# Windowed attention in plain 128-key blocks: 128x128 value products in place of 64-row pieces

## The chip, the cores and the metric

The kernel runs on one core of one Trainium2 chip. The metric is the device time of one execution in microseconds (us). A core has five engines that run side by side and wait for each other through semaphores: TensorE (PE in the profile; PEld is its row for loading the stationary operand), VectorE (DVE), ScalarE (ACT), GpSimd (POOL) and SyncE (SP). Transfers between DRAM and the on-chip memory are issued here from the queues of SP and POOL.

## The reference

Four batches of eight heads, 768 positions, 64 elements a head. Attention looks back over a window of 128 positions and always also at the first four positions (the sinks); a small expert layer then replaces 128 chosen rows of each batch.

```
scores = (q @ k.T) / 8
keep   = (pos_k < 4) | ((pos_q - pos_k >= 0) & (pos_q - pos_k < 128))
a      = softmax(where(keep, scores, -1e9))
x      = a @ v                                  # [4, 768, 512] with heads side by side
s      = x @ w_gate                             # one score a row
top    = the 128 rows of each batch with the largest s
out    = x;  out[top] = x[top] + sigmoid(s[top]) * (relu(x[top] @ w1) @ w2)
```

## The kernel before

**Units.** The attention is cut into blocks of 128 queries. A full unit is one block of one batch with all eight heads. Batches 1 to 3 have six full units each. Batch 0 is done in two halves of four heads, so it has twelve half units. That makes 30 units in all, in the list `steps`. The loop at L595 goes through them. In unit i it issues the scores of unit i+2 (`step_scores`), then the value products of unit i (`values`), then the normalisation (`norm`), and then what was hung on that unit by `at`, `late` and `before`: transposes of the keys and queries of the next batch, the scores for the sinks, ranks, the choice of rows, and the expert layer of an earlier batch. Every engine works its list in this order.

**Scores (L201 to L248).** Keys lie along the partitions of the output and queries along its columns. `scores(b, kc, gi)` makes four heads at a time: `a` chooses the head pair, `e` the head in the pair. Each block of 128 keys is made as two products of 64 keys (`m`), each with a window of 192 queries. They are 64x64 tiles of the PE array, so four of them, in different quarters of the array, can be in flight. For the second head pair (`a == 1`, heads 4 to 7) the block starts 64 keys earlier than for the first: the keys of these heads are shifted by half a block. The masks are added by more products with an identity matrix (L226, and L239, L245 at the first and last block). They touch only the two 64-column pieces of each window that are cut by the causal edge or by the window's far edge. ScalarE then takes the exponential of the 128x1024 result into a buffer `pt` (L248), in fp32.

**Values (L250 to L285).** The output has queries along the partitions and, for each head, 64 value columns plus one of ones that gives the softmax sum: 65 columns, fp32. The queries of a block are made as two halves `c`, which are the two column halves of the PE array. For each half a window of keys is covered by one product of all 128 key rows (`FULL`) and by two of 64 rows (`LO` and `HI`). So a head has two 128-row products and four of 64 rows in two array quarters each. An fp32 product is two matmul instructions in the profile, each with its own load of the stationary operand (`pt`).

**Sinks.** The four sink keys of each head are copied into `ksk` (L178). `sink_scores` (L185) makes their scores for a whole batch, for both query halves side by side, and ScalarE puts the exponential into `psk`. In `values` four products (`be`, `c`) of 64 rows, one in each array quarter, add the sinks' part (L264 to L272), with the sinks' values in `vsk`. `vsk` is filled at the start by four transfers on POOL's queue (L441), by DVE (L590), and by a copy on POOL (L592).

**Storage of the values.** There are two pairs of value buffers. In the second of a pair the keys are shifted by 64, which needs one more block. `load_v` (L140) issues two transfers a block on SP's queue, and `load_v_first` (L152) loads batch 0.

**Results of the products.** The scores alternate between two pairs of PSUM banks (`SC`). The value products of all units go to the same pair of banks (`X`), so the products of unit i+1 wait until `norm` of unit i has read it. `spread` (L312) broadcasts the scores of 128 rows by one fp32 product with a stationary operand of 128x128; it isn't touched by the change.

## Time and profile before

| | |
|---|---|
| median of 3 runs | 160.05 us (159.14 to 161.59) |
| the profiled execution, its own time | 160.06 us |
| its span, first to last instruction | 158.3 us |
| mean granted TensorE clock | 0.916 of full speed |
| busy: PE, DVE, ACT, POOL | 79%, 58%, 50%, 47% of the span |
| value products, L259 | 1440 matmuls, 48.4 us busy |
| exponentials, L248 | 48 of 128x1024, 1031 ns each |
| sink products, L269 | 180 matmuls, 15.9 us busy |
| score products, L210 | 384 matmuls, 18.4 us busy |
| mask products, L226, L239, L245 | 240 matmuls |

A line of the profile's table of groups names the source line, the engine, the operation, output<-inputs by name, the tile of the PE array (rows\*columns), partitions x elements and type of the operand, and the count; then the busy time, the mean of one in ns, and the idle time ahead of it with what ended it. A line of the timeline has the start (us from the span's start), the duration from the first start to the last end, the engine, the group and how many instructions were merged into it. Matmuls overlap and their ends are modelled, so what a product costs is read from the distance of starts and not from the duration of one. "issue" stands for idle time that ended without a releaser that the profile shows.

### The profile page before, as it was taken

The page shows a single profiled execution, that of the slowest core. Times are in us where ns is not written, and L with a number is a line of the kernel's source. Part 1 is how long each engine was busy: PE and PEld are TensorE (multiplying, and loading weights), DVE is VectorE, ACT ScalarE, POOL GpSimd, SP SyncE. Part 2 cuts the span into 40 slices and gives each one's busy share as a digit, 9 for nine tenths or more (in the row PEclk, how much of TensorE's full clock was granted, in tenths as well). Part 3 has the DMA queues.
Part 4 walks back from the last instruction along what each step waited for, and adds up shares of the span by engine and source line. Part 5 has one row for each costly group of instructions (what it writes and reads, how often), then busy time and mean ns, then how long its engine had stood idle before and what let it go on. Part 6 is the DMA issues. An engine that isn't in the chain of part 4 may idle for free. (4 is left out here: it accounts for less than half of the span.)

```text
span 158.3 us, 6368 instructions
## 1 busy us (share of the span) xinstructions
PE 125.5 (79%) x2756; PEld 95.2 (60%) x2756; DVE 91.2 (58%) x281; ACT 79.2 (50%) x106; POOL 75.1 (47%) x123
## 2 busy tenths in 40 slices
PE   6759797979499988578999997968299999889400
PEld 2236585757368867455787786756297785768100
DVE  6560344377424744129799896888982674783100
ACT  3248646559448785471878487747026642223100
POOL 8717799999399290149006046401051270602220
PEclk9965999999957999969999999999959999999975
DMA  4968979999979999799552743999440431110211
GB/s 157 300 139 276 301 256 253 391 377 368 341 173 340 324 363 331 187 268 261 172 153 59 242 136 76 187 215 229 106 133 4 137 133 70 66 70 12 86 42 60
DMA packets 36795, 30.85 MB, mean 195 GB/s; under 512 B 26896, under 2 KB 30352, under 8 KB 36768
## 3 DMA queue, kind: packets, MB, share of 16 engines
q1 hardware_dynamic: 31712, 16.79, 37.7%
q0 software_dynamic: 5056, 13.67, 28.8%
q8 instruction: 21, 0.34, 0.9%
q14 instruction: 6, 0.05, 0.1%
HBM read 25.20 MB, written 7.35 MB: 206 GB/s over the span
## 5 line engine op out<-in xcount | busy, mean ns | idle before, releaser
L259 PE MATMUL ps<-vbuf,pt 64*64 64x65 f32 (+1 forms) x1440 | 48.4, 231 | 8.0 <-issue 7.2
L259 PEld LDWEIGHTS ps<-vbuf,pt 64*64 64x64 f32 (+1 forms) x1440 | 41.2, 140 | 20.1 <-issue 16.5
L248 ACT ACTIVATE pt<-ps 128x1024 f32<-128x1024 f32 x48 | 47.3, 1031 | 6.8 <-PE ps L226 6.6
L292 DVE RECIPROCAL rz<-ps 128x8 f32<-128x8 f32 (+1 forms) x30 | 5.9, 197 | 38.1 <-PE ps L259 38.0
L138 POOL CAST kq<-raw 128x768 bf16<-128x768 f32 x28 | 23.2, 861 | 2.4 <-DMA raw<-in_q_dram 1.0
L183 POOL COPY ksk<-KT 64x4 bf16<-64x4 bf16 x32 | 7.3, 227 | 30.8 <-DVE KT L174 19.2
L210 PE MATMUL ps<-QT,KT 64*64 64x192 bf16 (+2 forms) x384 | 18.4, 258 | 2.7 <-ACT QT L176 1.7
L295 DVE TENSOR_TENSOR x<-ps,rz 128x256 f32<-128x256 f32 (+1 forms) x60 | 19.5, 366 | 1.2
L299 DVE CUSTOM_DVE_ANT_0 junk<-x,wgb 128x512 f32<-128x512 f32 x24 | 19.0, 792 | 0.4
L269 PE MATMUL ps<-vsk,psk 64*64 64x260 f32 (+1 forms) x180 | 15.9, 360 | 2.8 <-DVE x L295 2.8
L226 PE MATMUL ps<-mask,ident_b 64*64 64x256 bf16 (+1 forms) x208 | 16.5, 280 | 1.5 <-issue 1.5
L169 PE MATMUL ps<-ident_b,kq 128*128 128x128 bf16 x192 | 15.0, 231 | 2.8 <-DVE kq L138 2.4
L176 ACT COPY QT<-ps 128x768 bf16<-128x768 bf16 x16 | 12.8, 801 | 8.1 <-PE ps L169 8.1
L309 DVE TENSOR_SCALAR_CACHE_REDUCE junk<-sbc,scol 128x768 bf16<-128x768 f32 x12 | 12.1, 1012 | 6.6 <-DMA sbc<-srow 6.2
L210 PEld LDWEIGHTS <-KT 64*64 64x64 bf16 x384 | 10.7, 111 | 7.9 <-issue 4.6
L169 PEld LDWEIGHTS <-kq 128*128 128x128 bf16 x192 | 12.1, 103 | 5.2 <-DVE kq L138 3.4
L367 POOL DMA_INDIRECT xe<-out_dram,idx x4 | 4.9, 1218 | 20.8 <-DVE gt L358 15.8
L399 POOL DMA_INDIRECT out_dram<-y,idx x4 | 4.2, 1052 | 13.6 <-issue 6.4
L269 PEld LDWEIGHTS ps<-vsk,psk 64*64 64x64 f32 x180 | 7.4, 140 | 4.5 <-DVE x L295 3.2
L226 PEld LDWEIGHTS <-ident_b 64*64 64x64 bf16 x208 | 8.8, 117 | 1.7 <-issue 1.7
L174 DVE COPY KT<-ps 128x768 bf16<-128x768 bf16 x10 | 9.5, 951 | 0.1
L385 PE MATMUL ps<-xeT,w_sb 128*128 128x128 bf16 x128 | 9.1, 236 | 0.0
(84 smaller groups left out, 151.5 us busy)
## 6 DMA issues: line engine op xcount, KB each, us to landing
out_dram<-x SPq DMA_DIRECT2D x24, 256.0 KB, 4.3
raw<-in_k_dram POOLq DMA_DIRECT2D x12, 384.0 KB, 7.1
raw<-in_q_dram POOLq DMA_DIRECT2D x12, 384.0 KB, 7.8
vbuf<-in_v_dram SPq DMA_DIRECT2D x33, 128.0 KB, 5.4
w_sb<-in_moe_w_dram POOLq DMA_DIRECT2D x4, 512.0 KB, 10.4
raw<-in_k_dram SPq DMA_DIRECT2D x4, 384.0 KB, 3.4
raw<-in_q_dram SPq DMA_DIRECT2D x4, 384.0 KB, 5.5
vbuf<-in_v_dram SPq DMA_DIRECT2D x2, 384.0 KB, 7.7
```

The costliest lines, as they stand in the source:

```text
L138: (eng or pool).tensor_copy(out=o, in_=i)
L169: pe.transpose(out=trp[:, c, :], in_=src[:, c, :, :].rearrange("p h d -> p (h d)"), identity=ident_b[:, :])
L174: dve.tensor_copy(out=o, in_=i)
L176: act.copy(out=o, in_=i)
L210: pe.matmul(out=sc[64 * m:64 * m + 64, e, a, o:o + n], lhsT=s.KT[r, hp, k0:k0 + 64], rhs=s.QT[r, hp, k0:k0 + n], start=a == 0, stop=False, ...
L226: pe.matmul(out=o, lhsT=ident_b[r, r], rhs=w[r].unsqueeze(1).to_broadcast((64, a.stop - a.start, 2, 64)), start=False, stop=True, skip_gro ...
L248: act.activation(out=po[:, gi, :, :, :], in_=sc[:, :, :, :], func=ACT.Exp, scale=0.125)
L259: pe.matmul(out=ps[64 * c:64 * c + 64, bank + be, hh * SK:hh * SK + SK], lhsT=p[i][rows, h, 64 * slot:64 * slot + 64], rhs=s.v[be][rows, h ...
L269: pe.matmul(out=ps[64 * c:64 * c + 64, bank + be, a * SK:z * SK], lhsT=s.psk[which][r, c, 64 * (j - 1):64 * j], rhs=vsk[r, b, be, a:z, :], ...
L295: dve.tensor_tensor(out=xo[:, e, :, :], in0=xg[:, e, :, 0:D], in1=rz[:, e, 0:n, :].to_broadcast((128, n, D)), op=ALU.mult)
L299: dve.tensor_tensor_reduce(out=junk[:, :], in0=x, in1=wgb[:, :], scale=1.0, scalar=0.0, op0=ALU.mult, op1=ALU.add, accum_out=st[b].scol[:, ...
L309: dve.tensor_scalar(out=junk[:, :].bitcast(BF16)[:, 0:S], in0=sbc[:, :], scalar1=st[b].scol[:, c:c + 1], scalar2=0.0, op0=ALU.is_gt, op1=A ...
```

## The change

The keys are no longer shifted for heads 4 to 7, and the pieces of 64 are put together:

- Scores: one product for a head and block, 128 keys by 256 queries (128 in the last block). These are 64x128 tiles of the array. The masks are full: the four mask products of a call each cover all 256 queries of two heads, 512 columns, with zeros where nothing is masked. They stay 64x64 tiles. The special cases of the first and last block go.
- Values: two products of 128 rows for a head, with the 128 queries of the block as the stationary operand. These are 128x128 tiles. The first block of a batch has one product a head.
- Sinks: two products of 32 rows a unit, each with 128 queries. `sink_scores` writes both pieces to the same 64 partitions, where before two lay side by side on 128.
- `vsk` has half its columns, is filled by eight transfers on POOL's queue, and the copy of L592 goes; the selections for `own4` on POOL go from two to four.
- One value buffer of eight heads a batch: one transfer a block. The exponential of the last block has half the columns.

The core of the diff:

```diff
+    vbuf = [one([128, H, NB, VS], FP32, f"vbuf{i}") for i in range(2)]
+    vsk = one([64, B, HP, SK], FP32, "vsk")
+    mask = one([128, 3, 4, 64], BF16, "mask")
...
     def load_v(b, c):
...
+        return sp.dma_start(out=st[b].v[:, :, c, 0:D], in_=v[b, :, c * 128:(c + 1) * 128, :].rearrange("h p d -> p h d"))
...
     def sink_scores(b, hps, which, bank):
         s = st[b]
         for hp in hps:
...
-            for c in range(2):
-                o = 64 * (g ^ c)
-                q2 = s.QT[:, hp, 128:S].rearrange("p (j c n) -> p j c n", c=2, n=64)[:, :, c, :]
-                pe.matmul(out=ps[o:o + 64, bank + c, 0:320], lhsT=s.ksk[:, hp, :], rhs=q2,
-                          start=hp == mine[0], stop=hp == mine[-1], skip_group_check=True)
...
+            for n in range(2):
+                pe.matmul(out=ps[0:64, bank + n, 0:320], lhsT=s.ksk[:, hp, :], rhs=s.QT[:, hp, 128 + 320 * n:448 + 320 * n],
+                          start=hp == hps[0], stop=hp == hps[-1], skip_group_check=True)
...
     def scores(b, kc, gi):
...
-            for m in range(2):
-                k0 = kc * 128 - 64 * a + 64 * m
-                if k0 >= 0:
-                    for e in range(2):
-                        score(m, e, a, k0, 64 * m, min(W3, S - k0))
...
+            hp = 2 * a + gi
             for e in range(2):
...
+                r = slice(64 * e, 64 * e + 64)
+                pe.matmul(out=sc[:, e, a, 0:n], lhsT=s.KT[r, hp, k0:k0 + 128], rhs=s.QT[r, hp, k0:k0 + n],
+                          start=a == 0, stop=False, skip_group_check=True)
         for m in range(2):
             for e in range(2):
                 r = slice(64 * e, 64 * e + 64)
...
+                w = mask[r, 2 if kc == 0 and m == 0 else m, 0:n // 64, :].rearrange("p t n -> p (t n)")
+                pe.matmul(out=sc[64 * m:64 * m + 64, e, :, 0:n], lhsT=ident_b[r, r],
+                          rhs=w.unsqueeze(1).to_broadcast((64, 2, n)), start=False, stop=True, skip_group_check=True)
...
     def values(b, j, heads, bank, which):
...
+        if j:
+            for be in range(2):
+                r = slice(32 * be, 32 * be + 32)
+                pe.matmul(out=ps[:, bank + be, a * SK:z * SK], lhsT=s.psk[which][r, 128 * (j - 1):128 * j],
+                          rhs=vsk[r, b, a:z, :], start=True, stop=False, skip_group_check=True)
         for hh in heads:
...
+            for be in range(2):
+                h = 4 * be + hh
+                for i in ((j - 1, j) if j else (j,)):
+                    q0 = 128 * (j - i)
+                    pe.matmul(out=ps[:, bank + be, hh * SK:hh * SK + SK], lhsT=ptn[(b, i)][:, h, q0:q0 + 128],
+                              rhs=s.v[:, h, i, 0:SK], start=j == 0 and hh == a, stop=False, skip_group_check=True)
...
-        for hh in range(HP):
-            r0 = NSINK * hh
-            pool.dma_start(out=vsk[r0:r0 + NSINK, :, :, hh, 0:D].rearrange("p b e d -> p (b e) d"), in_=v4[hh, 0:NSINK])
+        for h in range(H):
+            r0 = 32 * (h // 4) + NSINK * (h % 4)
+            pool.dma_start(out=vsk[r0:r0 + NSINK, :, h % 4, 0:D], in_=v[:, h, 0:NSINK, :].rearrange("b s d -> s b d"))
...
-        pool.tensor_copy(out=vsk[64:80, :, :, :, :].rearrange("p b e h d -> p (b e h d)"),
-                         in_=vsk[0:16, :, :, :, :].rearrange("p b e h d -> p (b e h d)"))
```

## Prediction

> **What bounds the kernel now.** I read the page's shares first.

> ```profile
> span 158.3 us, 6368 instructions
> PE 125.5 (79%) x2756; PEld 95.2 (60%) x2756; DVE 91.2 (58%) x281; ACT 79.2 (50%) x106; POOL 75.1 (47%) x123
> ```

> PE leads, but its busy time is modelled, so I looked at the waits, at one unit's timeline, and at the groups with shapes kept apart.

> ```profile
> DVE rz L292 <- PE ps L259: 38.0, 25, 5.1
> ...
> PEld ps L259 <- issue: 16.5, 33, 2.0
> ...
> PE ps L259 <- issue: 7.2, 5, 1.9
> ```

> DVE waits 38.0 us for value products. The PE's own idle time mostly ends with "issue", not with another engine: the larger waits of its matmul row for others sum to 7.6 us (x L295 2.8 and 0.6, QT L176 1.7, KT L174 0.7, ch L351 1.8). So TensorE sets the pace from about 14 to 138 us, and I cost the change in its time. A full unit:

> ```profile
> 118.69 0.14 PEld L210 LDWEIGHTS <-KT 64*64 64x64 bf16 x8
> ...
> 118.88 0.28 PE L226 MATMUL ps<-mask,ident_b 64*64 64x256 bf16 x4
> ...
> 119.15 0.28 PE L226 MATMUL ps<-mask,ident_b 64*64 64x256 bf16 x4
> ...
> 119.26 0.61 PE L269 MATMUL ps<-vsk,psk 64*64 64x260 f32 x8
> ...
> 119.80 1.64 PEld L259 LDWEIGHTS ps<-vbuf,pt 128*64 128x64 f32 x64 [0.39 <-issue]
> ...
> 121.51 0.22 PEld L348 LDWEIGHTS <-E 128*128 128x128 bf16 x6
> ```

> Two score calls take 0.57 us (118.69 to 119.26; one follows the other by 0.27), the sinks 0.54, the values 1.71. A half unit's values take 1.01 (19.77 to 20.78), with 32 instructions instead of 64. The difference, 0.70 us, is 16 products: eight 128-row ones that run two abreast and eight 64-row ones four abreast, with two instructions each, so 12 steps of **58 ns**. Entering and leaving the tile forms makes up the rest, 1.01 - 0.70 = 0.31.

> The row closest to the new value product is `spread`, fp32 with a 128x128 stationary operand:

> ```profile
> 84.24 0.30 PEld L313 LDWEIGHTS ps<-ident_f,scol 128*128 128x128 f32 x2
> 84.25 0.49 PE L313 MATMUL ps<-ident_f,scol 128*128 128x128 f32 x2
> ...
> 84.35 0.19 PEld L313 LDWEIGHTS ps<-ident_f,scol 128*128 128x128 f32 x1
> 84.46 0.10 PEld L169 LDWEIGHTS <-kq 128*128 128x128 bf16 x1
> ```

> The second load starts 0.11 us after the first (84.35 against 84.24), and nothing was streaming ahead of it. So a load of 128 fp32 columns takes **0.109 us** (the starts in the trace, to the ns).

> [...] L348's six bf16 loads take 0.22 us at 0.096 each, a step of 25 ns. [...] The twelve transposes from 84.57 end 0.83 later; the last starts 0.22 before that and streams 0.05, to 85.23, and the first 64\*64 load starts at 85.33: a drain of **0.10**. [...] The page's 21 "instruction" packets of 0.34 MB fit PE's 5512 instructions.

> A step of 58 ns for 65 fp32 columns, against 55 ns for 128 bf16 columns in the transposes ((0.67-0.10)/11 with the rounding), means that an fp32 column costs two columns' time.

> **The change part by part**, at full clock. Units: 15 full with j>0, 3 full with j=0, 10 half with j>0, 2 half with j=0.

> *Values.* Before: 15 x 1.71 + 3 x 1.69 (51.08 to 52.77) + 10 x 1.01 + 2 x 0.99 (29.67 to 30.66) = 42.8. After: 704 matmuls, each with a load of 128 fp32 columns. The stream of 65 columns (54 ns) hides under the next load, not the reverse, so the step is the load, 0.109. 704 x 0.109 = 76.7; drain and first load, less the overlap of the last, are 0.15 a unit, x 30 = 4.5. Sum 81.2, so **+38.4**. Bounds of the step: 0.058 (loads vanish, the stream remains) and 0.111 (2 ns more between steps). I take 0.109 since L313 measures this very load.

> *Scores and masks.* After, one call is: drain 0.10, load 0.03 to 0.05, two pairs of 256 bf16 columns 2 x 0.109, drain 0.10, load 0.03, four masks abreast with 512 columns 0.217; 0.69 in all. Two calls 1.38 against 0.67 (0.57 and a drain): +0.71; a half unit +0.29. Last blocks have half the columns and lose ten instructions: about +0.08 and +0.03. First blocks were dearer before: +0.61 and +0.26. Sum 12 x 0.71 + 8 x 0.29 + 3 x 0.61 + 2 x 0.26 + 0.3 = **+13.5**. No row shows a 64\*128 tile. Bounds: no drain between it and 64\*64 takes off 8; pairs that do not run abreast add 10.

> *Sinks.* Two passes of 260 columns (0.22 each) stay; 32-row tiles are a form of their own: drain 0.10 [...], 25 x 0.2 = **+5.0**. If the two row tiles don't run abreast, +9 more; if the form costs no drain, -2.5. *Sink scores:* 32 matmuls that ran in pairs, step 0.135 (74.53, eight in 0.73, 0.30 each), now all in one column half: 16 x 0.135 = **+2.2**.

> Sum on PE: **+59.1**. Everything added lies in PE's own order: behind longer masks the exponentials (ACT L248) start later, behind longer values DVE's L292, then the stores on SP and the next unit's sinks, which need bank X back; none of these is late for another reason.

> *Given back.* Matmuls fall from 2756 to 1700, so 13 blocks of instructions instead of 21. The "issue" waits in mid-group (L259 7.2, L226 1.5) are 8.7 us; I take 5 back, between 0 and 8.7. Waits for other engines (7.6) are covered by the longer scores and values: 6, between 0 and 7.6. After either, PE's own next load is what is late. The granted clock:

> ```profile
> 39.58:42.99 3.41, 1.70 (x40) 1.45 (x41) 1.80 (x11) 1.07 (x2) 0.75 (x5) 1.00 1.05 345
> 42.99:49.82 6.83, 6.35 (x106) 4.74 (x105) 2.02 (x5) 4.65 (x6) 6.76 (x10) 0.50 0.90 244
> 63.47:66.88 3.41, 1.52 (x48) 1.31 (x52) 0.54 (x2) 1.44 (x2) 0.76 (x2) 1.00 0.75 192
> 66.88:70.29 3.41, 3.25 (x70) 2.73 (x60) 0.04 (x1) 1.91 (x3) 0.94 (x3) 0.50 0.87 237
> ```

> In this table of stretches (PE, PEld, DVE, ACT, POOL, clock), a stretch with PE half idle is followed by half clock. Three such cases total 13.7 us at half clock, worth about 6.6; fewer stalls give 2 back.

> *At no cost.* POOL: eight `vsk` transfers instead of four, 0.685 each, end at 9.3 instead of 6.55; four selections of 0.2 follow, to 10.1; the next instruction, `sink_keys`, started at 10.22, waiting for KT. Uncovered, each late us would delay ksk, then the sink scores at 13.40. The rows land 6.6 later, near 15.9, before the first sink product (17.0). Without L592 (1.91) the casts at 14.66 still wait for their transfer. SP: fewer value transfers, same bytes; its stores still wait for DVE. ACT: eight exponentials halve, some 0.4 each, but ACT is 50% busy. DVE's changed fills at the start are ahead of casts whose transfers land later anyway; at worst 1 us.

> 158.3 + 59.1 - 13 = 204.4 span. The profiled execution took 160.06, 1.8 more than its span, and the median is 160.05, so 204.4 + 1.8 = **206**.

> **Rivals.** *Forecast, load-bound products:* 206, 0.68; its own range is 192 (no inner drains, all given back) to 219 (row tiles one after another).

> *Half clock:* a stream of 54 in a step of 109 keeps the array streaming half the time, and one more stall in such a stretch may be enough for half clock; at half clock the L313 loads at 115.05 were 0.17 apart. For: the table above. Against: the stretches that lost the clock had whole gaps of over 1.5 us. 0.17 / 0.109 is 1.56, so 28 us of PE work at half clock instead of full add 0.56 x 28 = 16: 222. Chance 0.20.

> *Loads hidden:* the product costs its stream, 58 ns. Values 704 x 0.058 + 6 = 46.9, +4.1 in place of +38.4: 172. Against: L313. Chance 0.08.

> *Price by count, on the other side:* 64 instructions in 1.71 us read as 27 ns an instruction whatever its width. If a 128-wide one costs 29 too, values take 704 x 0.029 + 6 = 26.4, -16.4: total 59.1 - 38.4 - 16.4 - 13 = -8.7, 151 and faster. It decides below 41 ns an instruction (where the values give the 8 back that the rest costs, net of what returns). For: half the instructions. Against: L313's 109. Chance 0.04.

> **How the numbers follow.** The measurement tells about 2% from no change. Faster is the count rival, 0.04; within 2% needs a price near 41 ns, 0.02; slower 0.94. The range 190 to 226 takes in the forecast's unknown drains and abreast pairs at both ends and most of the half-clock case; it leaves out the hidden loads.

> **What would show it.** Right: L259 x704 at 128\*128, 32 loads over 3.5 us in a full unit, PEld busy near PE; masks of 512 columns step 0.69 from call to call; fewer "issue" gaps; DVE waiting far over 38 us for L259. Wrong: 32 loads in under 2 us, or long stretches at clock 0.50.

## The result and the profile after

The changed kernel takes 195.05 us (median of four executions, 192.75 to 210.68) against 159.6 us beside it. The profiled execution took 193.31 us, with a span of 191.6. The ratio is 1.211, 95% interval 1.200 to 1.221, without the two longer executions, 196.78 and 210.68 us, which ran at mean granted clocks of 0.951 and 0.88 instead of 0.974. In the changed kernel L218 is the value product, L194 the score product, L200 the masks, L211 the sinks.

The page's shares, PE's granted clock over 40 slices, the shares of the chain of work that ended last, and the groups of the value products:

```profile
span 191.6 us, 4224 instructions
...
PE 171.5 (89%) x1696; PEld 131.9 (69%) x1700; DVE 89.1 (47%) x283; ACT 76.3 (40%) x106; POOL 75.1 (39%) x128
...
PEclk9969999999999999999999999999999999999985
...
PE 75%; DVE 9%; DMA 5%; issue 3%; ACT 3%; SPq 1%; POOLq 1%; ACTq 0%; DVEq 0%
...
L218 PEld LDWEIGHTS ps<-vbuf,pt 128*128 128x128 f32 x704 | 80.8, 192 | 7.4 <-issue 5.8
L218 PE MATMUL ps<-vbuf,pt 128*128 128x65 f32 x704 | 85.0, 277 | 0.0
```

There are 704 value matmuls where there were 1440, and they take longer. The other engines' busy times have hardly moved. The matmul row of L218 has no idle time ahead of it: the pieces of "issue" that interrupted L259 are gone. PEclk has one dip, at the start, and its end.

The waits, largest first:

```profile
DVE rz L226 <- PE ps L218: 80.2, 28, 5.6
```

DVE now stands 80.2 us for value products, against 38.0. TensorE makes up 75% of the chain that ended last, and no other engine over 9%. A full unit in the timeline:

```profile
96.94 0.11 PEld L194 LDWEIGHTS <-KT 64*128 64x128 bf16 x4
...
97.27 0.11 PEld L200 LDWEIGHTS <-ident_b 64*64 64x64 bf16 x4 [0.21 <-issue]
...
97.61 0.11 PEld L194 LDWEIGHTS <-KT 64*128 64x128 bf16 x4 [0.23 <-issue]
...
97.93 0.11 PEld L200 LDWEIGHTS <-ident_b 64*64 64x64 bf16 x4 [0.21 <-issue]
...
98.27 0.30 PEld L211 LDWEIGHTS ps<-vsk,psk 32*128 32x128 f32 x4 [0.23 <-issue]
...
98.91 3.65 PEld L218 LDWEIGHTS ps<-vbuf,pt 128*128 128x128 f32 x32 [0.34 <-issue]
...
102.47 0.30 PEld L247 LDWEIGHTS ps<-ident_f,scol 128*128 128x128 f32 x2
```

From start to start: two score calls 1.33 us (96.94 to 98.27), the sinks 0.64, the values 3.56. The 32 loads span 3.65 with 0.19 for the last, so the step is (3.65 - 0.19) / 31 = 0.112 us.

### The profile page after: what moved, and what is told of

Its sections match the earlier page's. It is cut to its first block, busy times and chain, and to the rows that moved or that the text cites. A ratio compares the mean times of both kernels' runs of the same rounds, so it can differ in the third digit from the quotient of the medians.

```text
span 191.6 us, 4224 instructions
## 1 busy us (share of the span) xinstructions
PE 171.5 (89%) x1696; PEld 131.9 (69%) x1700; DVE 89.1 (47%) x283; ACT 76.3 (40%) x106; POOL 75.1 (39%) x128
## 4 chain that ended last, share of the span: by engine, by line
PE 75%; DVE 9%; DMA 5%; issue 3%; ACT 3%; SPq 1%; POOLq 1%; ACTq 0%; DVEq 0%
PE ps L218 40%; PE ps L211 7%; PE ps L200 7%; PE ps L194 7%; PE ps L153 4%; DMA raw<-in_q_dram 4%; PE ps L326 3%; PE ps L173 3%; DVE x L229 2%; PE ps L319 2%; DVE G L254 2%; DVE junk L243 2%; DMA out_dram<-y,idx 1%; ACT KT L160 1%; ACT QT L160 1%
## 5 line engine op out<-in xcount | busy, mean ns | idle before, releaser
L218 PEld LDWEIGHTS ps<-vbuf,pt 128*128 128x128 f32 x704 | 80.8, 192 | 7.4 <-issue 5.8
L218 PE MATMUL ps<-vbuf,pt 128*128 128x65 f32 x704 | 85.0, 277 | 0.0
L203 ACT ACTIVATE pt<-ps 128x1024 f32<-128x1024 f32 (+1 forms) x48 | 43.9, 957 | 13.3 <-PE ps L200 12.9
L226 DVE RECIPROCAL rz<-ps 128x8 f32<-128x8 f32 (+1 forms) x30 | 5.9, 197 | 80.2 <-PE ps L218 80.2
L167 POOL COPY ksk<-KT 64x4 bf16<-64x4 bf16 x32 | 9.6, 299 | 49.1 <-DVE KT L158 33.1
L194 PE MATMUL ps<-QT,KT 64*128 64x256 bf16 (+1 forms) x192 | 19.1, 271 | 2.3 <-ACT QT L160 1.2
L200 PE MATMUL ps<-mask,ident_b 64*64 64x512 bf16 (+1 forms) x192 | 19.3, 392 | 0.0
L160 ACT COPY QT<-ps 128x768 bf16<-128x768 bf16 x16 | 12.8, 801 | 12.4 <-PE ps L153 12.4
L153 PE MATMUL ps<-ident_b,kq 128*128 128x128 bf16 x192 | 13.8, 220 | 3.9 <-DVE kq L136 2.3
L211 PE MATMUL ps<-vsk,psk 32*128 32x260 f32 (+1 forms) x100 | 15.9, 386 | 0.1
L301 POOL DMA_INDIRECT xe<-out_dram,idx x4 | 4.9, 1220 | 23.4 <-DVE gt L292 17.3
L194 PEld LDWEIGHTS <-KT 64*128 64x128 bf16 x192 | 6.0, 94 | 11.5 <-issue 7.1
L200 PEld LDWEIGHTS <-ident_b 64*64 64x64 bf16 x192 | 5.5, 104 | 9.2 <-issue 7.9
L211 PEld LDWEIGHTS ps<-vsk,psk 32*128 32x128 f32 x100 | 7.8, 182 | 5.0 <-issue 3.7
L550 POOL CAST x<-x 128x512 bf16<-128x512 f32 x6 | 4.3, 713 | 17.1 <-DVE x L229 16.2
```

The costliest lines, as they stand in the source:

```text
L153: pe.transpose(out=trp[:, c, :], in_=src[:, c, :, :].rearrange("p h d -> p (h d)"), identity=ident_b[:, :])
L160: act.copy(out=o, in_=i)
L167: pool.tensor_copy(out=s.ksk[r, hp, c0:c0 + NSINK], in_=s.KT[r, hp, 0:NSINK])
L194: pe.matmul(out=sc[:, e, a, 0:n], lhsT=s.KT[r, hp, k0:k0 + 128], rhs=s.QT[r, hp, k0:k0 + n], start=a == 0, stop=False, skip_group_check=True)
L200: pe.matmul(out=sc[64 * m:64 * m + 64, e, :, 0:n], lhsT=ident_b[r, r], rhs=w.unsqueeze(1).to_broadcast((64, 2, n)), start=False, stop=True ...
L203: act.activation(out=po[:, gi, :, :, 0:n], in_=sc[:, :, :, 0:n], func=ACT.Exp, scale=0.125)
```

## The experiments

**1. Value products in column halves.** Same products, but two narrow stationary operands in place of one wide one:

```diff
-                    pe.matmul(out=ps[:, bank + be, hh * SK:hh * SK + SK], lhsT=ptn[(b, i)][:, h, q0:q0 + 128],
-                              rhs=s.v[:, h, i, 0:SK], start=j == 0 and hh == a, stop=False, skip_group_check=True)
+                    for c in range(2):
+                        pe.matmul(out=ps[64 * c:64 * c + 64, bank + be, hh * SK:hh * SK + SK],
+                                  lhsT=ptn[(b, i)][:, h, q0 + 64 * c:q0 + 64 * c + 64],
+                                  rhs=s.v[:, h, i, 0:SK], start=j == 0 and hh == a, stop=False, skip_group_check=True)
```

> The changed kernel, with each value product of 128 queries issued as two products of 64 queries, one in each column half of the array (128x64 tiles); scores, masks and sinks stay as changed. Load theory (a product costs the load of its fp32 columns, 0.111 us for 128, and two loads of 64 run side by side): 704 steps of 0.058 instead of 704 of 0.111, 37 us less on PE; [...] so 156 to 168 us. Rival 1 (a product costs the same however wide it is): 704 more matmuls, 270 us. Rival 2 (the streams of the moving operand set the pace): no change, 193 us.

Measured: 165.17 us (164.45 to 167.04), 1.031 times the kernel before (1.022 to 1.041). It lies in the expected 156 to 168; the upper end allowed 12 us for "issue" gaps and half clock to come back, the author's estimate. The value group and one full unit's loads:

```profile
L219 PE MATMUL ps<-vbuf,pt 128*64 128x65 f32 x1408 | 47.7, 224 | 0.0
...
96.83 1.95 PEld L219 LDWEIGHTS ps<-vbuf,pt 128*64 128x64 f32 x64 [0.34 <-issue]
```

Twice the instructions in about half the time: 64 loads in 1.95 us, (1.95 - 0.14) / 31 = 0.058 us for a pair. Both rivals of this run fall. Nearly all of the loss, 30 of some 35 us, goes away when only the width of the stationary operand changes. The 0.0 at the end of the group line matters for another step: with 2404 matmuls and 19 instruction packets there is no "issue" gap ahead of a value matmul.

**2. A narrower stream.** In units with j>0 the products stream 33 of the 65 columns; half of the window's value columns are left out there.

```diff
+                    d0 = 32 if j else 0
-                    pe.matmul(out=ps[:, bank + be, hh * SK:hh * SK + SK], lhsT=ptn[(b, i)][:, h, q0:q0 + 128],
-                              rhs=s.v[:, h, i, 0:SK], start=j == 0 and hh == a, stop=False, skip_group_check=True)
+                    pe.matmul(out=ps[:, bank + be, hh * SK + d0:hh * SK + SK], lhsT=ptn[(b, i)][:, h, q0:q0 + 128],
+                              rhs=s.v[:, h, i, d0:SK], start=j == 0 and hh == a, stop=False, skip_group_check=True)
```

> The changed kernel, but in units with j>0 the value products stream 33 of the 65 columns (the other 32 value columns get only the sinks' part, so half of the window's values are left out); loads, count and order are the same. Load theory: the stream (54 ns, then 28) is hidden under the next load either way, so no change, 191 to 195 us. Stream theory: 640 matmuls lose half their price, 0.055 each, 35 us less, 158 us.

Measured: 275.67 us (259.46 to 279.66), which neither theory had. Less work took 80 us more. Three stretches of its profiled execution (length, PE, PEld, DVE, ACT, POOL, then the clock), and the value loads of a full unit at full clock and of a half unit at half clock:

```profile
50.81:54.22 3.41, 3.41 (x18) 3.34 (x17) 0.00 (x0) 0.48 (x1) 2.62 (x4) 0.50 0.25 46
...
98.60:102.01 3.41, 3.41 (x35) 2.95 (x31) 2.25 (x5) 1.22 (x3) 0.76 (x2) 1.00 0.51 145
102.01:105.42 3.41, 3.41 (x23) 3.22 (x22) 1.10 (x4) 0.48 (x1) 0.00 (x0) 0.50 0.09 21
...
87.24 3.65 PEld L219 LDWEIGHTS ps<-vbuf,pt 128*128 128x128 f32 x32 [0.34 <-issue]
...
50.88 3.49 PEld L219 LDWEIGHTS ps<-vbuf,pt 128*128 128x128 f32 x16 [0.23 <-issue]
```

At full clock the 32 loads take 3.65 us, exactly as with 65 columns, so the stream does not set the step. But the execution's mean clock is 0.678. At half clock 16 loads take about what 32 take at full clock, a step of (3.49 - 0.33) / 15 = 0.21 us. The clock is lost at 102.01, behind a stretch in which the PE row is full. So it was not lost to idle time on that row. What the edit lowered is the share of time in which the array streams, an estimated 28 ns (33 columns at the 0.85 ns that the sinks give for one) in each 112. That is the half-clock rival of the forecast, which this run was not made to test and its expectation didn't name.

**3. The products in bf16.** Only the upper 16 bits of each number are read, so values and weights are cut to bf16, and with them the scores by which rows are chosen.

```diff
-                    pe.matmul(out=ps[:, bank + be, hh * SK:hh * SK + SK], lhsT=ptn[(b, i)][:, h, q0:q0 + 128],
-                              rhs=s.v[:, h, i, 0:SK], start=j == 0 and hh == a, stop=False, skip_group_check=True)
+                    w = ptn[(b, i)][:, h, q0:q0 + 128].bitcast(BF16).rearrange("p (n t) -> p n t", t=2)[:, :, 1]
+                    vb = s.v[:, h, i, 0:SK].bitcast(BF16).rearrange("p (n t) -> p n t", t=2)[:, :, 1]
+                    pe.matmul(out=ps[:, bank + be, hh * SK:hh * SK + SK], lhsT=w,
+                              rhs=vb, start=j == 0 and hh == a, stop=False, skip_group_check=True)
```

> The changed kernel, but the value products read only the upper 16 bits of each fp32 number, as bf16, of both operands (values and weights cut to bf16, so the scores of the rows and their choice can differ): 352 matmuls instead of 704, each with a load of 128 bf16 columns. If the price is the fp32 load: [...] the products take 10 to 19 us instead of 78, and PE alone stops being the bound: 130 to 150 us, with DVE (89 us busy) next. If each matmul keeps its price of 0.111: 39 us less, 154 us. If the step of a bf16 load with a stride isn't shorter than a load of fp32: also 154.

Measured: 151.81 us (150.43 to 153.02), 0.949 times the kernel before (0.938 to 0.960). The time alone would not separate the cases, since 154 was also the answer for an unchanged price. Two steps of bf16 loads of 128 columns stand in the trace before, 0.025 us (L348) and 0.056 (L169); 352 of them would take 9 to 20 us. The trace separates the cases:

```profile
94.24 0.57 PEld L220 LDWEIGHTS <-pt 128*128 128x128 bf16 x16 [0.34 <-issue]
```

Sixteen loads of 128 bf16 columns in 0.57 us, a step of (0.57 - 0.10) / 15 = 0.031, and half as many of them: a full unit's values take 0.6 us instead of 3.6. Other waits now hold the kernel up, and PE is no longer alone on the path:

```profile
PEld ps L211 <- DVE x L231: 9.6, 5, 8.5
DVE junk L245 <- DMA sbc<-srow: 9.5, 1, 9.5
```

DVE stood 9.5 us in one piece for the row scores' way through DRAM, and PE stood 8.5 behind it. The clock fell as well: it was at half from 61.4 to 75.1 us, from inside that wait on, and the mean was 0.872 to 0.883 in the four executions.

**4. Scores first, then masks.** In a full unit the order score, mask, score, mask becomes score, score, mask, mask, which saves two changes of the tile form:

```diff
-            for gi in ((0, 1) if g is None else (g,)):
-                scores(b, kc, gi)
+            scores(b, kc, (0, 1) if g is None else (g,))
...
+    def scores(b, kc, gis):
+        bodies = [score_parts(b, kc, gi) for gi in gis]
+        for part in range(2):
+            for body in bodies:
+                next(body, None)
```

> The changed kernel, but in a full unit both calls' score products come first and then both calls' masks, so that the tile form changes two times less in each of 18 full units. Drain theory (0.10 for a change of form and 0.02 for the uncovered load): 36 x 0.12 = 4.3 us less, 189 us. If the gap ahead of the masks is not the change of form: no change, 193 us.

Measured: 195.33 us (192.19 to 224.63), 1.212 times the kernel before (1.192 to 1.231): no clear difference from the changed kernel. The trace shows the local gain all the same, here at full clock; in this kernel L200 is the score product, L207 the masks, L218 the sinks:

```profile
96.24 0.61 PE L200 MATMUL ps<-QT,KT 64*128 64x256 bf16 x8
96.78 0.63 PE L207 MATMUL ps<-mask,ident_b 64*64 64x512 bf16 x8
97.34 0.71 PE L218 MATMUL ps<-vsk,psk 32*128 32x260 f32 x4
```

The two calls take 1.10 us (96.24 to 97.34) instead of 1.33. So 64\*128 and 64\*64 are two forms, and each of the two changes saved had cost 0.11 (0.23 / 2), the load that comes uncovered with it included. Eighteen units would give 4 us. The profiled execution had a clock of 0.802 and took 224.63 us. But the clock doesn't hide the 4 us: executions of this kernel and of the changed one (experiment 5) at the same clock, 194.44 us at 0.961 against 195.03 at 0.960 and 192.19 at 0.970 against 192.81 at 0.972, are 0.6 us apart. Where the rest went isn't settled.

**5. A wider stream, and the changed kernel again beside it.** Three of four value products stream their 65 columns twice, the second time 256 columns further on. The added columns of the first head begin at column 256 and the last head's end at 259, so the first four of them are added to the last head's results, other than the expectation says.

```diff
+                    if hh < 3:
+                        o = ps[:, bank + be, :].rearrange("p (t n) -> p t n", t=2)[:, :, hh * SK:hh * SK + SK]
+                        x = x.unsqueeze(1).to_broadcast((128, 2, SK))
+                    pe.matmul(out=o, lhsT=w, rhs=x, start=j == 0 and hh == a, stop=False, skip_group_check=True)
```

> The changed kernel, but three of four value products stream their 65 columns twice, the second time into columns of the bank that nobody reads (work added, nothing left out): 130 fp32 columns, 108 ns[...]. Load theory: the second stream is free, the step goes from 0.111 to at most 0.115, and the executions stay within 190 to 196 us. Half-clock theory on top: the array now streams most of the time in the value products, so the granted clock stays at 0.97 in every execution and the long executions of the changed kernel (197 to 225) are gone. Stream theory: 528 matmuls gain 54 ns each, 28 us more, 221 us.

> The changed kernel itself beside the wide one on the same chip: 192 to 197 us in most executions, longer ones where the granted clock is lower. If the half clock comes from stretches in which the array streams half the time, some of its executions show it here too and none of the wide kernel's do.

Measured: 194.6 us (191.47 to 197.99), 1.218 times the kernel before (1.206 to 1.230), against 195.41 us (192.72 to 196.58) and 1.221 (1.209 to 1.233) for the changed kernel itself. The wide kernel's groups and one full unit's loads:

```profile
L223 PE MATMUL ps<-vbuf,pt 128*128 128x130 f32 x528 | 67.0, 279 | 0.0
...
99.74 3.65 PEld L223 LDWEIGHTS ps<-vbuf,pt 128*128 128x128 f32 x32 [0.34 <-issue]
```

The loads take 3.65 us again. Twice the streamed columns cost nothing, and half of them gained nothing: the stream is wholly under the load. The half-clock part of the expectation is not borne out: two of the wide kernel's six executions had a clock of 0.954. Both kernels had 0.95 to 0.98 here, and neither had an execution over 198 us, so the two can't be told apart by it.

**6. Halves and order together.**

> The changed kernel with the value products in column halves and with both calls' scores ahead of both calls' masks. The order takes 0.22 us off two calls in the trace of the fourth experiment (1.10 against 1.33), 18 full units: 4 us less than the halves alone, so 161 us. If PE's waits for DVE or ACT take the gain: 165 us.

Measured: 164.08 us (159.47 to 168.21, clocks of 0.932 to 0.970). The four spread over 9 us, so the order's gain on top of the halves (165.17) is not shown. In fp32 no version came clearly under the kernel before.

**7. bf16, order, and batch 0's ranks one unit later.** The part added to experiments 3 and 4:

```diff
-                late(i + 2 + min(c, 4), lambda b=b, c=c: rank_c(b, c))
+                late(i + (3 + min(c, 3) if b == 0 else 2 + min(c, 4)), lambda b=b, c=c: rank_c(b, c))
```

> Value products from the upper 16 bits as bf16 (both operands cut, so the scores of the rows and their choice can differ), scores ahead of masks, and batch 0's comparisons of ranks one unit later, so that DVE does not stand 9.5 us for the round trip of the scores through DRAM, with PE behind it for 8.6. If that stand was on the path: 8 us less than the bf16 products alone and some 2 for the order, 141 to 144 us. If another wait ends as late: 150 us.

Measured: 148.36 us (146.18 to 150.64), 0.926 times the kernel before (0.916 to 0.936), below the 151.81 of experiment 3 but short of the 141 to 144 expected. What the order and the later ranks each gave isn't separated. One line of its waits shows what is left:

```profile
DVE junk L252 <- DMA sbc<-srow: 6.5, 1, 6.5
```

The wait shrank from 9.5 to 6.5 and did not go. In a faster kernel one unit is not long enough for that way through DRAM. It is the fastest version here, with the precision named above.

## Why the prediction was right, and where it was off

The forecast was 206 us, load-bound; 195.05 was measured, in the lower part of its range (190 to 226) and of the forecast's own 192 to 219. The mechanism was right, and most of its sums were somewhat too high. The table compares the steps; before and after are distances of starts in the traces. For the sums, the distances of successive matmuls are added by the group of the earlier one, from 12 us to the last matmul, with what exceeds 0.30 us of a gap over 0.46 counted as waiting.

| step | forecast | measured |
|---|---|---|
| step of a value matmul | 0.109 | 0.112 |
| values, full unit | 1.71 to 3.64 | 1.71 to 3.56 |
| two score calls | 0.67 to 1.38 | 0.57 (no 0.10 for a change of form added here) to 1.33 |
| sinks, full unit | +0.20 | 0.54 to 0.64 (the change of form ahead of them counts with the masks) |
| values, sum | +38.4 | 46.6 to 80.8, +34.2 |
| scores, masks and sinks, sum | +18.5 | 33.1 to 45.6, +12.5 |
| sink scores, sum | +2.2 | 3.6 to 4.9, +1.3 |
| waiting of PE | -11 | 16.4 to 5.1, -11.3 |
| start of the last matmul | | 147.61 to 181.72 |

*The load.* Right, by three runs: half the width took nearly all of the loss away (1), half the stream (2, at full clock) and twice the stream (5) changed nothing. The pair of L313, 0.109 apart, showed only the first step of a series, which is shorter: in the changed kernel 0.108 and then 0.112, at half clock (2) 0.167 and then 0.213. So a load at half clock costs 1.9 times as much, not the 1.56 of the half-clock rival.

*A column of fp32.* The forecast read the step of 58 ns before as the stream of 65 columns. In experiment 1 a pair of 64-column loads follows the last one after 58 ns too, so that step does not tell stream from load. The sinks do: a full unit's take 0.22 more than a half unit's (0.64 against 0.42) for 130 more columns in each of two passes, 0.85 ns a column, where 512 bf16 columns (L326) take 0.216 us, 0.42 a column. So 65 fp32 columns take an estimated 55 ns (65 x 0.85).

*Scores, masks, sinks.* Right in kind: a change of form costs about 0.1, also between 64\*128 and 64\*64 (0.11 in experiment 4). What the forecast calls a drain is such a gap of 0.10 us; the traces show its length, not what fills it. The forecast's 0.20 for a unit's sinks is the author's estimate of this gap and a load, for which 0.109 (L313) is the nearest measured figure. Row tiles ran abreast: the two of a pair start 7 ns apart (L211; before, the four mask tiles of L226 started 3 to 4 ns apart and took 0.27 us each), and the four sink matmuls, 0.22 each, take 0.64 with the load ahead of them, and one after another they would take an estimated 0.88 without it. For a full unit +0.76, +0.10 and +1.85 make 2.71, where 0.71, 0.20 and 1.93 made 2.84. More of the error lies in half units, in first and last blocks and in short waits, which the sums hold too; it was not taken apart.

*Given back.* The waits came back in sum as forecast, 11.3 against 11, but that is luck. The "issue" waits went away whole, 8.7 where 5 were taken, and those for other engines shrank by 2.6 where 6 were taken.

*Where 12.8 us of the forecast span went.* Between 12 us and the last matmul the kernel before spent 17.3 us at half clock (3.7 up to 15.7 us, then the 13.7 of the forecast), the changed one 2.3. Compared with each group's mean step at full clock, the work in these stretches took an estimated 6.1 us more before and 0.4 after. So the clock gave back 5.7, where 2 were taken. With this taken out of the sums, scores, masks and sinks rose by 13.8 instead of 18.5, values by 36.2 instead of 38.4, and sink scores by 2.2 as forecast. Of the 12.8 us, 4.7 are then the scores, masks and sinks, 3.7 the clock, 2.2 the values, 1.0 other products, 0.8 the stretch behind the last matmul (10.7 to 9.9), and 0.4 the waits and the start. This account is worked out from the two traces and not tested by a run.

*Why the "issue" gaps went.* The forecast tied them to the number of instruction blocks, the "instruction" packets of the page's queue q8. These follow the number of PE's instructions: 21 for 5512 before, 13 for 3396 after, 262 and 261 to a packet. The gaps are gone with 13 packets, but also in experiment 1 with 19, against 21 before. So the count alone does not explain them. The trace before does show a tie: all six PE gaps over 0.9 us that end with "issue" begin within 0.35 us of the end of an instruction packet (the one at 39.34 us has a packet from 38.39 to 39.53). Experiment 6, with 19 packets, has two gaps of this kind (0.9 and 1.8 us), each about half a microsecond from the end of a packet. Why most packets pass without a gap stays open.

*The half-clock rival.* Half clock on such a scale occurs: experiment 2 had mean clocks of 0.613 to 0.678, and single executions of two kernels (210.68 at 0.88; 224.63 at 0.802) show its price. In nine of ten executions the changed kernel had a mean clock of 0.95 or more, streaming an estimated 55 ns in each 112. How near that is to losing the clock is in the last section.

*Loads hidden, price by count.* Both fall: the step was 0.112, where they needed 0.058 and under 0.041. For the count: before, a head has two products of 128 rows and two of 64 (the description of the values counts four), which with two instructions each makes the 64 of a full unit.

*At no cost.* The first sinks were issued at 17.44, not held up by the eight transfers; the fourth POOL selection ended at 8.5, and `sink_keys` started at 10.46.

## What to carry to other kernels

Count what a product costs by the longer of two things, the load of its stationary operand and its stream, not by the number of products. Here a load of 128 fp32 columns set a step of 0.112 us over an estimated 55 ns of stream, and a stream of 512 bf16 columns (L326) set one of 0.216 over loads that elsewhere followed each other after 0.025 to 0.056. With 128 fp32 columns to load and 65 to stream, joining two narrow products into one wide one nearly doubled their time (1.95 us a unit in experiment 1, 3.65 in the changed kernel), because two loads of 64 columns run side by side in the two column halves (in the trace before, the two of a pair at L259 start 6 to 7 ns apart and take 138 ns each). Before widening a stationary operand, find the distance of loads of that width and type in a trace, in a series rather than in one pair. If the precision allows it, a bf16 operand takes away most of that cost (0.031 us from load to load against 0.112, and one instruction instead of two).

## What the runs showed of the hardware that was not expected

In experiment 2 TensorE lost half its clock behind a stretch in which its row was busy for all 3.41 us: with an estimated 28 ns of streaming in each 112 ns the mean granted clock fell to 0.61 to 0.68 and the kernel took 275.67 us, for less work than the 195.05 us of the changed kernel. The load itself slowed with the clock, from 0.112 to 0.21 us for 128 fp32 columns.
